# Fourier mixing and an MLP mixer on one core: where the residual adds, the block sums and the edge copies of the second channel product run

## The chip, the cores and the metric

The kernel runs on one NeuronCore of one Trainium2 chip. The metric is the device time of one execution in microseconds. Three runs of the kernel before took 618.13, 616.25 and 618.18 us, with a median of 618.13 us.

## The reference

The input x is 8 batches of 3008 rows and 256 features. It goes through a Fourier mixing (the real part of a two-dimensional FFT over rows and features) and then through a mixer: a two-layer MLP over the rows (256 hidden units) that is added to its input, and a two-layer MLP over the features (1536 hidden units) that is added too.

```
def _attn_ref(x):
    X = np.fft.fft(np.fft.fft(x, axis=1), axis=2)
    return X.real
def _moe_ref(x, w_tok1, w_tok2, w_ch1, w_ch2):
    xt = x.transpose(0, 2, 1)
    h = np.maximum(xt @ w_tok1, 0.0) @ w_tok2
    u = x + h.transpose(0, 2, 1)
    h2 = np.maximum(u @ w_ch1, 0.0) @ w_ch2
    return (u + h2)
```

## The kernel before

**Batches, chunks and quarters.** The outer loop (L772) goes over the 8 batches b. A batch's u lies in SBUF turned (features on partitions) in six chunks of 512 rows (L775, `ut`). Each chunk is worked in four quarters s (L782); I call quarter s of chunk c "sub" 4c+s, 24 to a batch. In a quarter, `mm1` (L584) makes three of the twelve 128-unit tiles of the hidden layer of the present chunk: six matmuls of 512 columns into PSUM `pc`, and three relu copies by ScalarE into `c1` (L595).

**The second channel product.** `mm2` runs one chunk behind: in the same quarter it makes a quarter of the previous chunk's output. For 42 of the 48 chunks this is `mm2_sums` (L620), a product by halves with block sums (a Strassen-like scheme, with seven block products for eight). The other six chunks, "plain" ones (L581), use direct products (L690) and VectorE alone for their residual adds (L702).

In `mm2_sums` two PSUM banks `px` and `py` are kept for a whole chunk, and the four quarters use them in turn:

- s=0: two products from `c1` into `px`; ScalarE copies half of `px` out into `m` (`keep(0)`, L638); VectorE adds the other half and `m` into the output tile `osb` (L645); then GpSimd adds the residual u (tile `rt`) to the same 128x256 part of `osb` (L646).
- s=1: a product of the block sum `sb[0]` into `py`, one of `sb[1]` into `px`, and `keep(1)`.
- s=2: a product of `c1` into `px`, `keep(2)`, and VectorE's add from `py` and `m` (L654). The part of `c1` that it reads has been overwritten by a block sum.
- s=3: a product into `px`, one of `sb[2]` into `py`, two adds by VectorE (L658, L659); then GpSimd adds the residual to the whole upper half of `osb`, 128x512 (L660), and SyncE writes `osb` out in two DMAs (L664).

**Block sums.** `block_sums` (L599) are four adds on VectorE for each half of a chunk's hidden tiles, 128x768 in fp16, all inputs in SBUF: sum 0 makes `sb[0]` from `c1`, sum 1 makes `sb[1]` from `sb[0]` and `c1`, sum 2 overwrites part of `c1` from `c1`, sum 3 makes `sb[2]` from `c1` and `sb[1]`. The first half of a chunk's sums is made in its own quarters s=2 (sums 0 and 1) and s=3 (sums 2 and 3), after that quarter's `mm2` (L792). The second half is made in the next chunk's s=0 and s=1, straight after `mm1` and ahead of everything else of the quarter (L786).

**Residual tile and edges.** `rt` is u turned back by two transposing DMAs on SyncE's queue (L575). `edges` (L611) fixes one or two columns of it, a 128x4 copy each on VectorE, at the start of the chunk's `mm2`.

**What sets the order.** The schedule is written by hand (`manual_schedule`): each engine executes in the order in which the code issues to it. Between the steps, pieces of the next batch's front (`front`, L436: `pz`, `pw`, `pt`, `py`/`pq`, `pu`, all from a ring of three PSUM banks) and of the present batch's own front are taken by the numbers of `plan` and `own_plan` (L765 to L769); the fold of a later batch (L414, adds on VectorE) is taken in at the end of quarters (L811). `load_x` (L122), six DMAs from GpSimd's queue, waits for the last fold step of the batch before. The tile framework puts semaphore waits where one engine reads what another writes.

The lines that matter for the order, in quarter s:

```
                mm1(b, c, c1, range(3 * s, 3 * s + 3))
                if s < 2 and prev is not None and not plain(*prev[0:2]):
                    block_sums(prev[2], pbox["sb"], slice(3, HC), (2 * s, 2 * s + 1))
                take(own, own_plan[b > 0][sub])
                take(nxt, n // 2)
                if prev is not None:
                    mm2(*prev, s, pbox)
                if s >= 2 and not plain(b, c):
                    block_sums(c1, box["sb"], slice(0, 3), (2 * s - 4, 2 * s - 3))
                ...
                take(nxt, n - n // 2)
```

Of the kernel before, what the change touches and what calls it, by code (L numbers as in the profile page):

```python
# [40 lines left out]
def kernel(  # L41
# [9 lines left out]
    nc = tc.nc  # L51
# [17 lines left out]
    def ps_out(name):  # L69
        return psum.tile([P, 512], FP32, tag="o2", name=name, bufs=2)  # L70
# [4 lines left out]
    def dram(t, offset, ap):  # L75
        return bass.AP(tensor=t, offset=offset, ap=ap)
# [84 lines left out]
    for t in (tp, tq):  # L161
        for i in range(2):
            h = slice(64 * i, 64 * i + 64)
            nc.scalar.activation(
                out=t[h, :, 64 - 64 * i:128 - 64 * i],
                in_=pcol[h, :].unsqueeze(2).to_broadcast([64, NG, 64]),
                func=AFT.Copy, scale=0.0)
    nc.scalar.activation(out=w1m[64:128, NG - 1, :],
                         in_=pcol[64:128, :].to_broadcast([64, DTOK]),
# [52 lines left out]
    HC = NCT // 2  # L222
# [184 lines left out]
    def align_w2(j):  # L407
        th, k = j // 4, slice(16 * (j % 4), 16 * (j % 4) + 16)
        copy(0, w2p[:, th, k, 0:NQ], w2v[:, th, k, :])
# [161 lines left out]
    def turn_u(b, c):  # L571

        rt = work.tile([P, 4, D + 16], FP16, tag="rt", name="rt", bufs=4)
        for h in range(2):
            nc.sync.dma_start_transpose(  # L575
                out=rt[:, :, h * P:(h + 1) * P], in_=state[b]["ut"][c][:, h, :])
        return rt
# [3 lines left out]
    def plain(b, c):  # L581
        return (b, c) == (0, 0) or c + 1 == NCH and (b % 2 == 0 or b + 1 == BB)
# [16 lines left out]
    def block_sums(c1, sb, k, which):  # L599
        hi = slice(HC + k.start, HC + k.stop)  # L600
        a11, a21 = c1[:, k, 0:D], c1[:, k, D:CW]
        a12, a22 = c1[:, hi, 0:D], c1[:, hi, D:CW]
        sums = ((sb[:, 0, k], a21, a22, AT.add),
                (sb[:, 1, k], sb[:, 0, k], a11, AT.subtract),
                (a21, a11, a21, AT.subtract),
                (sb[:, 2, k], a12, sb[:, 1, k], AT.subtract))
        for i in which:
            o, x, y, op = sums[i]
            nc.vector.tensor_tensor(out=o, in0=x, in1=y, op=op)  # L609

    def edges(rt, c):  # L611
        for o, i in ((D, 0), (0, P)) if c >= 3 else ((D, P),):
            nc.vector.tensor_copy(out=rt[:, :, o:o + 1], in_=rt[:, :, i:i + 1])

    lower, upper, turned_ = slice(0, P), slice(P, D), slice(D, P, -1)

    def residual(eng, o, x, y):
        eng.tensor_tensor(out=o, in0=x, in1=y, op=AT.add)  # L618

    def mm2_sums(b, c, c1, s, box):  # L620
        if s == 0:
            box["osb"] = work.tile([P, 4, D], FP32, tag="osb", name="osb", bufs=3)
            box["m"] = work.tile([P, 3, 2, P], FP32, tag="m", name="m")
            box["po"] = ps_out("px"), ps_out("py")
            edges(box["rt"], c)
        osb, rt, sb, m = (box[i] for i in ("osb", "rt", "sb", "m"))
        pa, pb = (p[:].rearrange("p (i t d) -> p i t d", i=2, t=2) for p in box["po"])

        def product(o, a, hi, w, first=False):
            for t in range(2):  # L630
                f = D * hi + P * t
                for k in range(HC):
                    nc.tensor.matmul(o[:, t], lhsT=a(k)[:, f:f + P], rhs=w(k),  # L633
                                     start=(first and t == 0 and k == 0),
                                     stop=(k == HC - 1), skip_group_check=True)

        def keep(i):
            nc.scalar.activation(out=m[:, i], in_=pa[:, 0], func=AFT.Copy)  # L638

        v, g = nc.vector, nc.gpsimd  # L640
        if s == 0:
            product(pa[:, 0], lambda k: c1[:, k], 0, lambda k: wc2[:, k, lower], True)
            product(pa[:, 1], lambda k: c1[:, HC + k], 0, lambda k: wc2[:, HC + k, lower])
            keep(0)
            residual(v, osb[:, 0:2, lower], pa[:, 1], m[:, 0])  # L645
            residual(g, osb[:, 0:2, lower], osb[:, 0:2, lower], rt[:, 0:2, lower])  # L646
        elif s == 1:
            product(pb[:, 0], lambda k: sb[:, 0, k], 0, lambda k: wst[:, 0, k], True)
            product(pa[:, 0], lambda k: sb[:, 1, k], 0, lambda k: wst[:, 1, k])
            keep(1)  # L650
        elif s == 2:
            product(pa[:, 0], lambda k: c1[:, k], 1, lambda k: wst[:, 2, k])
            keep(2)
            residual(v, osb[:, 2:4, upper], pb[:, 0], m[:, 2])  # L654
        else:
            product(pa[:, 0], lambda k: c1[:, HC + k], 1, lambda k: wst[:, 3, k])
            product(pb[:, 0], lambda k: sb[:, 2, k], 0, lambda k: wc2[:, HC + k, upper])
            residual(v, osb[:, 2:4, lower], pa[:, 0], rt[:, 2:4, lower])  # L658
            residual(v, osb[:, 0:2, upper], pb[:, 0], m[:, 1])  # L659
            residual(g, osb[:, :, upper], osb[:, :, upper], rt[:, :, turned_])  # L660
        if s == 3:
            for i in range(2):
                nk = 3 if c + 1 == NCH and i else 4
                nc.sync.dma_start(  # L664
                    out=dram(out_t, (b * S + 8 * c + i) * D,
                             [[NQ * D, 64], [2 * D, nk], [1, D]]),
                    in_=osb[64 * i:64 * i + 64, 0:nk, :])
            if c + 1 == NCH:
                nc.sync.dma_start(
                    out=dram(out_t, ((b - 1) * S + NQ - 1) * D, [[NQ * D, 64], [1, D]]),  # L670
                    in_=osb[64:P, 3, :])

    def mm2(b, c, c1, ks, box):
        if not plain(b, c):
            return mm2_sums(b, c, c1, ks, box)
# [41 lines left out]
    def pair(b, c1):  # L717

        if b % 2 == 0 and b + 1 < BB:
            state["ch"] = work.tile([P, NCT, 64], FP16, tag="ch", name="ch")  # L720
            nc.vector.tensor_copy(out=state["ch"][:], in_=c1[:, :, CW - 128:CW - 64])
        elif b % 2:
            nc.vector.tensor_copy(out=c1[:, :, CW - 64:CW], in_=state["ch"][:])


    def take(g, n):
        for _ in range(n):
            next(g, None)
# [41 lines left out]
    prev = None  # L770
    turned_u = {(0, 0): turn_u(0, 0)}
    for b in range(BB):  # L772
        nxt = front(b + 1) if b + 1 < BB else iter(())
        folds = fold(b + 2, [nc.vector] * 4) if b + 2 < BB else None
        for c in range(NCH):  # L775
            c1 = work.tile([P, NCT, CW], FP16, tag="c1", name="c1", bufs=2)
            box = {"rt": turned_u.pop((b, c))}
            if not plain(b, c):
                box["sb"] = work.tile([P, 3, HC, D], FP16, tag="sb", name="sb", bufs=2)
            if c + 1 == NCH and b % 2:  # L780
                pair(b, c1)
            for s in range(4):  # L782
                sub = 4 * c + s
                n = plan[b > 0][sub]
                mm1(b, c, c1, range(3 * s, 3 * s + 3))
                if s < 2 and prev is not None and not plain(*prev[0:2]):  # L786
                    block_sums(prev[2], pbox["sb"], slice(3, HC), (2 * s, 2 * s + 1))
                take(own, own_plan[b > 0][sub])
                take(nxt, n // 2)
                if prev is not None:  # L790
                    mm2(*prev, s, pbox)
                if s >= 2 and not plain(b, c):  # L792
                    block_sums(c1, box["sb"], slice(0, 3), (2 * s - 4, 2 * s - 3))
                if b == 0 and sub < 16 and sub % 2:
                    align_w2(sub // 2)
                take(nxt, n - n // 2)
                if s == 2 and c + 1 < NCH:
                    turned_u[b, c + 1] = turn_u(b, c + 1)
                if s == 3 and c + 1 == NCH and b + 1 < BB:
                    turned_u[b + 1, 0] = turn_u(b + 1, 0)  # L800
                if b == 0 and sub == 4:
                    weight_sums()
                if b == 0 and sub == 3:
                    for h in range(2):
                        swap_wc1(h)
                if b == 0 and 3 <= sub < 9:
                    take(early, 2)
                    if sub == 8:
                        x_tiles[2] = load_x(2)
                if folds is not None and sub >= fold_at[b > 0]:  # L810
                    take(folds, 1 + (b == 0))  # L811
                    if sub == fold_at[b > 0] + (5 if b == 0 else 11) and b + 3 < BB:
                        x_tiles[b + 3] = load_x(b + 3)
            if c + 1 == NCH and b % 2 == 0:
                pair(b, c1)
            prev, pbox = (b, c, c1), box
        own = nxt
# [32 lines left out]
```

## Time and profile before

| what | value |
|---|---|
| median of three runs | 618.13 us |
| the profiled execution's own time | 616.26 us |
| its span, first to last instruction | 614.2 us |
| TensorE matmul (PE) busy | 589.1 us, 96% of the span |
| VectorE (DVE) busy | 492.8 us, 80% |
| ScalarE (ACT) busy | 442.0 us, 72% |
| GpSimd (POOL) busy | 139.3 us, 23% |
| GpSimd's 84 residual adds | 92.2 us |
| granted TensorE clock | 1.0 |

Busy time is the time in which at least one instruction of an engine was executing. A row of a group reads: source line, engine, operation, written tile <- read tiles, shapes, count | busy us, mean ns of one | idle us of the engine just before, and what ended it. A row of the timeline reads: start in us, length in us, engine, line, operation, tiles, shape, count, and in square brackets the idle time ahead of it. Matmul lengths overlap, since matmuls are pipelined: twelve matmuls of 128 columns follow each other in 0.67 us although each is shown with 219 ns. So TensorE's lost time is read from starts: a group should start when the group before it started, plus its count times its pitch.

### The profile page before, as it was taken

How to read it: one execution, taken by the hardware profiler on the slowest of the kernel's cores; microseconds unless marked ns; L12 is line 12 of the kernel's file. 1: busy time of each engine (PE TensorE's matmuls, PEld its weight loads, DVE VectorE, ACT ScalarE, POOL GpSimd, SP SyncE). 2: the span in 40 equal slices, each digit the busy share in tenths (PEclk: the TensorE clock that was granted, in tenths of full speed). 3: DMA queues.
4: the chain of work that ended last, by engine and by line, in shares of the span. 5: the costliest groups of instructions: out<-in, count | busy, mean ns of one | idle time of the engine just before them, and what ended most of it. 6: DMA issues, size and time to landing. Idle time of an engine off the chain costs nothing.

```text
span 614.2 us, 15694 instructions
## 1 busy us (share of the span) xinstructions
PE 589.1 (96%) x6322; PEld 422.5 (69%) x6322; DVE 492.8 (80%) x1086; ACT 442.0 (72%) x996; POOL 139.3 (23%) x163
## 2 busy tenths in 40 slices
PE   2899999999999999999999999999999999999996
PEld 1766767667776767767676777766776767766675
DVE  8768879668998699768988789857899778867684
ACT  8866986677767777686766767777777777667772
POOL 8500413111142121302114221311121212101121
PEclk9999999999999999999999999999999999999999
DMA  8994842725347323672419234392222433232433
GB/s 137 210 192 93 183 67 56 162 57 84 53 89 141 85 52 68 118 120 52 97 44 174 53 83 74 61 183 61 53 62 58 91 53 75 65 69 60 88 62 94
DMA packets 86600, 56.52 MB, mean 92 GB/s; under 512 B 54864, under 2 KB 83472, under 8 KB 85776
## 3 DMA queue, kind: packets, MB, share of 16 engines
q1 hardware_dynamic: 78048, 37.84, 30.9%
q0 software_dynamic: 8256, 17.49, 16.5%
q8 instruction: 49, 0.80, 0.5%
q10 hardware_dynamic: 224, 0.20, 0.1%
q14 instruction: 23, 0.19, 0.1%
HBM read 34.98 MB, written 24.64 MB: 97 GB/s over the span
## 4 chain that ended last, share of the span: by engine, by line
PE 80%; DVE 8%; ACT 6%; issue 3%; POOL 1%; DMA 1%; DVEq 0%; POOLq 0%
PE pc L592 33%; PE px L633 20%; PE py L633 7%; PE pu L552 6%; PE po L690 4%; PE pt L488 3%; ACT c L595 3%; DVE sb L609 2%; DVE osb L618 2%; PE pz L445 1%; PE pw L472 1%; PE pw L473 1%; DVE ut L560 1%; PE py L519 1%; DVE yt L526 1%
## 5 line engine op out<-in xcount | busy, mean ns | idle before, releaser
L595 ACT ACTIVATE c<-pc 128x512 f16<-128x512 f32 (+1 forms) x572 | 295.8, 594 | 39.2 <-PE pc L592 19.8
L618 POOL TENSOR_TENSOR osb<-osb,rt 128x256 f32<-128x256 f32 x84 | 92.2, 1097 | 438.5 <-DVE osb L618 411.4
L592 PE MATMUL pc<-ut,wc1p 128*128 128x512 f16 x576 | 140.3, 379 | 0.0
L592 PE MATMUL pc<-ut,wc1m 128*128 128x512 f16 (+1 forms) x576 | 134.9, 370 | 0.0
L633 PEld LDWEIGHTS <-c 128*128 128x128 f16 x2016 | 121.3, 98 | 19.4 <-issue 0.3
L633 PEld LDWEIGHTS <-sb 128*128 128x128 f16 x1512 | 90.2, 98 | 14.1 <-issue 5.0
L638 ACT ACTIVATE m<-px 128x256 f32<-128x256 f32 x126 | 48.6, 386 | 69.9 <-PE px L633 45.2
L592 PEld LDWEIGHTS <-wc1p 128*128 128x128 f16 x576 | 52.2, 98 | 49.0 <-issue 2.3
L560 DVE TENSOR_TENSOR ut<-pu,yt 128x512 f16<-128x512 f32 (+1 forms) x96 | 64.1, 669 | 26.1 <-PE pu L552 26.1
L592 PEld LDWEIGHTS <-wc1m 128*128 128x128 f16 x576 | 53.0, 98 | 46.3
L609 DVE TENSOR_TENSOR sb<-c,sb 128x768 f16<-128x768 f16 x84 | 84.4, 1004 | 0.0
L633 PE MATMUL px<-wst,c 128*128 128x128 f16 x1008 | 70.0, 219 | 0.0
L633 PE MATMUL px<-wc,c 128*128 128x128 f16 x1008 | 63.1, 219 | 0.0
L618 DVE TENSOR_TENSOR osb<-py,m 128x256 f32<-128x256 f32 x84 | 35.4, 422 | 29.4 <-ACT m L638 23.2
L290 ACT ACTIVATE z<-pz 128x480 f16<-128x480 f32 (+1 forms) x60 | 40.1, 672 | 19.4 <-PE pz L445 12.4
L552 PE MATMUL pu<-w2p,uu 128*128 128x512 f16 (+1 forms) x168 | 50.0, 379 | 0.0
L609 DVE TENSOR_TENSOR c<-c 128x768 f16<-128x768 f16 x84 | 49.5, 590 | 0.0
L609 DVE TENSOR_TENSOR sb<-sb,c 128x768 f16<-128x768 f16 x84 | 46.9, 558 | 2.9
L609 DVE TENSOR_TENSOR sb<-c 128x768 f16<-128x768 f16 x84 | 45.9, 547 | 2.4 <-ACT c L595 2.4
L475 DVE SCALAR_TENSOR_TENSOR w<-alt,pw 128x131 f16<-128x131 f16 x96 | 33.0, 350 | 14.4 <-ACT w L290 14.3
L633 PE MATMUL px<-wst,sb 128*128 128x128 f16 x504 | 34.9, 219 | 3.2 <-DVE osb L618 2.6
L526 DVE TENSOR_TENSOR yt<-py,qs 128x512 f16<-128x512 f32 x48 | 30.8, 683 | 8.8 <-ACT qs L522 8.8
(163 smaller groups left out, 674.3 us busy)
## 6 DMA issues: line engine op xcount, KB each, us to landing
out_dram<-osb SPq DMA_DIRECT2D x83, 256.0 KB, 3.7
xp<-in_x_dram POOLq DMA_DIRECT2D x16, 272.0 KB
out_dram<-osb SPq DMA_DIRECT2D x11, 192.0 KB, 3.2
xp<-in_x_dram POOLq DMA_DIRECT2D x16, 127.5 KB
rt<-ut SPq DMA_TRANSPOSE x96, 3.4
w2s<-in_moe_w_tok_dram POOLq DMA_DIRECT2D x1, 1504.0 KB
w1p<-in_moe_w_tok_dram POOLq DMA_DIRECT2D x2, 384.0 KB
wc<-in_moe_w_ch_dram POOLq DMA_DIRECT2D x1, 768.0 KB
```

Of the source, the lines that this page charges most:

```text
L290: nc.scalar.activation(out=out_, in_=in_, func=AFT.Copy)
L475: nc.vector.scalar_tensor_tensor(out=w[:, g, 0:131], in0=alt[:], scalar=pw[:, 131:132], in1=pw[:, 0:131], op0=AT.mult, op1=AT.add)
L526: nc.vector.tensor_tensor(out=yt[:, h, CW * c:CW * c + CW], in0=py[:], in1=qs[:], op=op)
L552: nc.tensor.matmul(pu[:, 0:n], lhsT=uu[:, th, int(minus), h, :], rhs=w2_cols(b, c)[:, th], start=(th == 0), stop=(th == 1))
L560: nc.vector.tensor_tensor(out=ut[:, h, 0:n].rearrange("p (a b) -> p a b", b=64), in0=pu[:, 0:n].rearrange("p (b a) -> p a b", b=64), in1=y ...
L592: nc.tensor.matmul(pc[:, 0:n], lhsT=wc[:, h, ct * P:(ct + 1) * P], rhs=ut[:, h, 0:n], start=(h == 0), stop=(h == 1))
L595: nc.scalar.activation(out=c1[:, ct, 0:n], in_=pc[:, 0:n], func=AFT.Relu)
L609: nc.vector.tensor_tensor(out=o, in0=x, in1=y, op=op)
L618: eng.tensor_tensor(out=o, in0=x, in1=y, op=AT.add)
L633: nc.tensor.matmul(o[:, t], lhsT=a(k)[:, f:f + P], rhs=w(k), start=(first and t == 0 and k == 0), stop=(k == HC - 1), skip_group_check=True)
L638: nc.scalar.activation(out=m[:, i], in_=pa[:, 0], func=AFT.Copy)
L690: nc.tensor.matmul(po[0:n, o:o + D], lhsT=c1[:, ct, ks * P:ks * P + n], rhs=wc2[:, ct, :], start=(ct == 0), stop=(ct == NCT - 1))
```

## The change

Three things change.

1. The two residual adds of a chunk that GpSimd made (L646 and L660) are made by VectorE: `g` becomes `nc.vector`.
2. The edge copies (L613) go from VectorE to GpSimd.
3. The block sums are issued at other places of the quarter. In s=0 (second half, sums 0 and 1) they come after the first pieces of the fronts, just ahead of `mm2`. In s=1 (second half, sums 2 and 3) they come last, after `mm2` and the remaining pieces of the front. In s=2 (first half, sums 0 and 1) they stay behind `mm2`. In s=3 (first half, sums 2 and 3) they come straight after `mm1`, ahead of `mm2`.

```
     def edges(rt, c):
         for o, i in ((D, 0), (0, P)) if c >= 3 else ((D, P),):
-            nc.vector.tensor_copy(out=rt[:, :, o:o + 1], in_=rt[:, :, i:i + 1])
+            nc.gpsimd.tensor_copy(out=rt[:, :, o:o + 1], in_=rt[:, :, i:i + 1])
...
-        v, g = nc.vector, nc.gpsimd
+        v, g = nc.vector, nc.vector
...
                 mm1(b, c, c1, range(3 * s, 3 * s + 3))
-                if s < 2 and prev is not None and not plain(*prev[0:2]):
-                    block_sums(prev[2], pbox["sb"], slice(3, HC), (2 * s, 2 * s + 1))
+                def now():
+                    which = 2 * (s % 2), 2 * (s % 2) + 1
+                    if s >= 2 and not plain(b, c):
+                        block_sums(c1, box["sb"], slice(0, 3), which)
+                    elif s < 2 and prev is not None and not plain(*prev[0:2]):
+                        block_sums(prev[2], pbox["sb"], slice(3, HC), which)
+
+                if s == 3:
+                    now()
                 take(own, own_plan[b > 0][sub])
                 take(nxt, n // 2)
+                if s == 0:
+                    now()
                 if prev is not None:
                     mm2(*prev, s, pbox)
-                if s >= 2 and not plain(b, c):
-                    block_sums(c1, box["sb"], slice(0, 3), (2 * s - 4, 2 * s - 3))
+                if s == 2:
+                    now()
                 if b == 0 and sub < 16 and sub % 2:
                     align_w2(sub // 2)
                 take(nxt, n - n // 2)
+                if s == 1:
+                    now()
```

The instructions of TensorE, ScalarE and SyncE, and their order, are the same in both kernels. GpSimd keeps its setup work and its DMA issues, loses 84 adds and gains 72 copies; VectorE gains the 84 adds and loses the 72 copies.

## Prediction

> **What bounds the kernel now.** I read the page first: engine shares and the chain that ended last.
>
> ```profile
> PE 589.1 (96%) x6322; PEld 422.5 (69%) x6322; DVE 492.8 (80%) x1086; ACT 442.0 (72%) x996; POOL 139.3 (23%) x163
> ...
> PE 80%; DVE 8%; ACT 6%; issue 3%; POOL 1%; DMA 1%; DVEq 0%; POOLq 0%
> ```
>
> TensorE is busy nearly all the time and makes 80% of the chain; VectorE makes 8% and ScalarE 6%, the places where TensorE had to wait. Next, who TensorE waited for:
>
> ```profile
> PE px L633 <- DVE osb L618: 2.6, 8, 0.8
> PE pz L445 <- DVE ut L560: 1.6, 3, 0.7
> PE pt L488 <- DVE w L475: 1.1, 1, 1.1
> ```
>
> The columns are us in total, times, longest. These count only idle time between modelled ends. To size the real stalls I went through all matmuls in order of start and compared each start-to-start distance with the pitch of undisturbed groups (12 products of 128 columns in 0.67 us, six of 512 in 1.29 us). After 60 us, distances more than 0.06 us too long add up to 13.6 us. Of these `px<-wst,sb` (the second product of quarter s=1) has 5.6 us in 15 places, `pz` 2.1 us in 3, `pt<-w` 1.95 us in 7. The other 3.9 us are mostly small matmuls of L455 to L461, which have nothing to do with the change. So VectorE can give back 9.7 us at most. Before 60 us and after the last matmul nothing of the change lies.
>
> What makes VectorE late shows in the timeline around one such place:
>
> ```profile
> 312.62 0.55 DVE L609 TENSOR_TENSOR c<-c 128x768 f16<-128x768 f16 x1
> 312.79 1.41 POOL L618 TENSOR_TENSOR osb<-osb,rt 128x512 f32<-128x512 f32 x1 [7.00 <-DVE osb L618]
> 313.09 1.52 DVE L609 TENSOR_TENSOR sb<-c,sb 128x768 f16<-128x768 f16 x1
> ...
> 317.94 0.83 PE L633 MATMUL py<-wst,sb 128*128 128x128 f16 x12
> 318.12 0.38 DVE L613 COPY rt<-rt 128x4 f16<-128x4 f16 x2
> 318.85 0.42 DVE L618 TENSOR_TENSOR osb<-px,m 128x256 f32<-128x256 f32 x1 [0.35 <-ACT c L595]
> ...
> 319.33 0.83 PE L633 MATMUL px<-wst,sb 128*128 128x128 f16 x12 [0.56 <-DVE osb L618]
> ```
>
> GpSimd's 128x512 add runs from 312.79 to 314.20, and VectorE's block sum beside it takes 1.52 us. Five us later `py` starts at 317.94 and is due to end its issue at 317.94 + 0.67 = 318.61, but `px<-wst,sb` starts at 319.33: it waits for the add at 318.85 that reads the same bank, and that add stands behind block sums and edge copies in VectorE's queue. The groups by shape tell how much time goes this way:
>
> ```profile
> L609 DVE TENSOR_TENSOR sb<-c,sb 128x768 f16<-128x768 f16 x84 | 84.4, 1004 | 0.0
> L609 DVE TENSOR_TENSOR c<-c 128x768 f16<-128x768 f16 x84 | 49.5, 590 | 0.0
> L609 DVE TENSOR_TENSOR sb<-sb,c 128x768 f16<-128x768 f16 x84 | 46.9, 558 | 2.9
> L609 DVE TENSOR_TENSOR sb<-c 128x768 f16<-128x768 f16 x84 | 45.9, 547 | 2.4 <-ACT c L595 2.4
> ...
> L613 DVE COPY rt<-rt 128x4 f16<-128x4 f16 x72 | 13.3, 184 | 0.8
> ...
> L245 DVE TENSOR_TENSOR gr<-gv,mp 128x768 f32<-128x768 f32 x1 | 1.0, 959 | 0.0
> ...
> L245 DVE TENSOR_TENSOR gr<-gv,m 94x120 f32<-94x120 f32 x1 | 0.3, 280 | 0.0
> ```
>
> ```profile
> L618 POOL TENSOR_TENSOR osb<-osb,rt 128x512 f32<-128x512 f32 x42 | 60.3, 1437 | 241.8 <-DVE osb L618 237.1 <-DVE rt L613 4.7
> L618 POOL TENSOR_TENSOR osb<-osb,rt 128x256 f32<-128x256 f32 x42 | 31.8, 758 | 196.6 <-DVE osb L618 174.3 <-DMA out_dram<-osb 22.3
> ```
>
> The four block sums have the same shape and type, but take 547, 558, 590 and 1004 ns. Instruction by instruction, VectorE operations after 45 us are 53.8 us longer than the undisturbed ones of their shape: 38.5 us in `sb<-c,sb`, 3.6 in `c<-c`, 9.7 in the fold, the rest in copies. Every one of them overlaps a GpSimd residual add.
>
> [...] block sums (both inputs in SBUF) are stretched by 1.0 us, the adds from PSUM (423 ns) never. [...]
>
> **The change, part by part.**
>
> Adds to VectorE: 42 of 256 and 42 of 512 elements, both inputs in SBUF, not shown in the trace on this engine. Between the L245 rows (120 elements 280 ns, 768 elements 959) the slope is 1.05 ns, so 0.42 and 0.69 us[...]. Lower bound 0.41 and 0.68 (the same sizes from PSUM, L618 and L560), upper 0.45 and 0.72 with the 0.034 us seen ahead of an operation that waits for its forerunner. Sum 42 x 1.11 = 46.6 us of VectorE. The s=0 add stands behind the add that TensorE waits for, the s=3 add behind both adds that free `px` and `py`. It delays what follows: front pieces and the next sums.
>
> Adds off GpSimd: the 53.8 us of contention go. Edge copies off VectorE: 72 x 0.184 = 13.3 us. VectorE: 492.8 + 46.6 - 53.8 - 13.3 = 472 us. Little in sum; what counts is where. At the end of s=3, behind the adds from PSUM, stood sum 2 (0.55) and a sum 3 of 0.55 to 2.04 us; now the 0.69 us add stands there, and the two sums run ahead, while TensorE still makes the products that those adds await. VectorE enters s=0 about 1.3 us earlier where there was contention, and its queue to the critical add is 0.17 to 0.38 us of copies shorter.
>
> I followed the stretch above with measured durations, queued operations 0.08 us closer than their length, as in the timeline. Sums 2 and 3 end by 311.84, the adds from PSUM by 312.7, the residual add at 313.3 (before, sum 3 at 314.61). The two `yt` operations wait for ScalarE's `qs` (315.99) and end at 317.3; two sums end at 318.3, the critical add at 318.62. `py` issues until 318.61, so `px` waits about 0.1 us, not 0.72. Likewise at 329.98, where `pz` loses 0.88 us behind a sum of 2.04 us, `ut` ends at 328.45 and `pz` is due at 328.5. So I leave 0.8 of the 5.6 us, 0.4 of the 2.1 and 0.85 of the 1.95: in the `pt` case at 97.39 the last `w` now stands behind the 0.69 us add, not behind 1.1 us of sums. Gain 4.8 + 1.7 + 1.1 = 7.6 us.
>
> New wait one: in s=1 sum 2 (`c<-c`) now comes last, and the product of s=2 needs it from its fourth weight on. Where a `w` or `ut` of the same quarter stands ahead of it, it can't start early. That holds in 13 chunks with `w` (subs 9 and 17 of six batches, and one of the first) and about 7 with `ut` (sub 21). At 306.5 ScalarE's `w` ends 306.52, VectorE's `w` takes to 306.9, `c<-c` 306.83 to 307.37; the fourth weight is due at 307.22 + 3 x 0.058 = 307.40. Just late; at 285.4 the same sum gives 0.08 us late. I take 0.1 us x 13 = 1.3 us; the `ut` case has 0.07 us to spare in the stretch above. Bounds: 0 and 0.3 us each, 0 to 6 us. Behind the waiting matmul stands all of TensorE.
>
> New wait two: VectorE's s=0 add waits for GpSimd's edge copies, and behind it stands all of VectorE. GpSimd now does little else, so the copies run as soon as `rt` lands, chunks ahead. The exception is behind `load_x`: at the two batch boundaries after 60 us where block sums follow, its issues end at 183.25 and 327.70, and the next critical add at 188.5 and 332.9. About 5 us to spare, for two copies: nothing. If that cover were gone, those places would lose what is missing, one for one.
>
> Edge copies on GpSimd: its rows on 128x1 tiles last 0.19 to 0.64 us, so 72 cost 14 to 46 us of an idle engine. [...] I take 0.2 us and nothing on the path, the other end is rival B. SyncE's output DMAs wait for an add that ends 0.9 us earlier; nothing is queued longer.
>
> Sum: 7.6 - 1.3 = 6.3 us. Against the profiled execution, 616.26 - 6.3 = 610.0 (span 607.9). The median of the runs lies 1.9 us above that execution (two runs at 618.1, one at 616.25), so for the median **618.13 - 6.3 = 611.8 us**.
>
> **The rivals.**
>
> B, [...] After the change two-input VectorE work is 185 us of sums, 47 of adds and 52 of fold, 46% of the span. 72 copies of 0.64 us would block 21 us. Before, 53.8 us blocked cost at most 9.7, under a fifth: 3.8 us. Time 611.8 + 3.8 = 615.6. For it: a copy was itself stretched to 1.16 us beside a GpSimd add, so the engines do collide. Against: four elements a partition are a tenth of the add's work or less.
>
> C, slower: sum 2 is late. Its place at the end of s=1, the 20 chunks above, is the mechanism; the price is the lateness of `c<-c` to TensorE, in full. For it: the working above has no margin. Against: it is late by hundredths when the queue ahead is empty. It decides from 7.6 / 20 = 0.38 us each: there the gain is used up (618). If VectorE brings a backlog of its own into these quarters, say 0.75 us each, it is 618.1 - 7.6 + 15 = 625.5 us.
>
> That the change doesn't do what it says is ruled out by the order of instructions, which shows 84 adds and 72 copies on their new engines, TensorE's order untouched.
>
> **How the numbers follow.** Forecast 0.60 (608 to 614.5; from lateness 0 to 0.3 us and 0 to 4 us of the old stalls left), B 0.17 (614.5 to 617), C 0.23, of which 0.06 end within 0.3% (up to 619) and 0.17 above. 0.3% of 618.13 is 1.9 us, about what this measurement can tell from no change. B splits at 616.3 into 0.10 faster, 0.07 same. So faster 0.70, same 0.13, slower 0.17. The range 608 to 618.5 holds the forecast, B and C's small end.
>
> **What would show it.** Right: `sb<-c,sb` at 0.55 us, VectorE 472 us busy, `px<-wst,sb` stalls below 1 us, TensorE's excess after 60 us near 7 us. Wrong: `px<-wst,c` waiting for VectorE's `c` in subs 10, 18 and 22 (C); two-input operations of VectorE still stretched, beside edge copies (B); VectorE idle until GpSimd's `rt` at batch boundaries.

## The result, and the profile after

The changed kernel takes 611.87 us (median of four runs, 611.84 to 613.79), the kernel before 617.82 us beside it. The ratio is 0.9916, with a 95% interval of 0.9890 to 0.9942: faster by 0.6% to 1.1%. The profiled execution took 611.84 us, with a span of 610.1 us.

**The spread of the traces comes from the set-up.** Both kernels' times lie between a lowest value and some 2 us above it (before: 616.25 to 618.18). The traces of all kernels of this study show where: the first `pc` matmul starts at 38.4 us in some executions and as late as 40.5 us in others, whatever the kernel. The two lines below, from the changed kernel and from run `e10_one_w_first`, show the same 24 `filler` matmuls of L283:

```profile
21.41 1.50 PE L283 MATMUL filler<-anti,ident 128*128 128x128 f16 x24
```

```profile
22.18 2.76 PE L283 MATMUL filler<-anti,ident 128*128 128x128 f16 x24
```

From start to start they take 0.056 us each in the first trace and 0.107 us in the second.

So beside the ratio I use the time from the first `pc` matmul to the end of the trace, the main part, which is free of this: 575.8 us before, 571.6 us after, 4.1 us less. Up to the first place that an edit reaches, 48.5 us into the main part, the matmuls of all 13 traces of this study start within 0.003 us of each other. The profiled executions differ by 4.4 us (616.26 and 611.84), of which 0.3 us lies outside the span: 616.26 - 614.2 = 2.1 us before, 611.84 - 610.1 = 1.7 us after.

The page of the changed kernel, engine shares and chain:

```profile
PE 587.2 (96%) x6322; PEld 420.8 (69%) x6322; DVE 478.0 (78%) x1098; ACT 442.3 (72%) x996; POOL 66.6 (11%) x151
...
PE 83%; DVE 2%; issue 0%; DVEq 0%
```

These shares add up to only 85%, because the chain is followed back no further than 88.1 us here; in the kernel before it goes back into the set-up, so the two lists can't be compared as they stand. From 88.2 us on, VectorE makes 35.0 us of the chain before and 9.5 us after, ScalarE 25.5 us and none, and from 98 us on VectorE makes 0.3 us: there TensorE alone holds the end. Who TensorE still waited for (us in total, times, longest):

```profile
PE pt L488 <- DVE w L475: 1.4, 1, 1.4
...
PE py L633 <- DVE sb L609: 0.3, 1, 0.3
...
PE px L633 <- DVE osb L618: 0.2, 1, 0.2
PE px L633 <- DVE c L609: 0.2, 1, 0.2
```

The 2.6 us of `px` behind the add from PSUM have gone down to 0.2, `pz` behind `ut` is gone; one wait of `pt` for the last `w` is left, 1.4 us long, and has grown from 1.1. (Waits of the set-up are left out.) Measured as in the prediction, start to start, TensorE's excess after 60 us fell from 13.6 to 9.1 us: `px<-wst,sb` 5.6 to 1.35, `pz` 2.1 to 0, `pt<-w` 1.95 to 2.4, and two that were not there, `px<-wst,c` 1.4 in 12 places and one `py<-wst,sb` of 0.47. The excess fell by 4.5 us and the main part by 4.1; the rest is in delays of 0.06 us or less, which the excess doesn't count.

The stretch that the prediction followed, in the trace after (start us, us, engine, line, operation, tiles, shape, count):

```profile
309.46 0.55 DVE L609 TENSOR_TENSOR c<-c 128x768 f16<-128x768 f16 x1
309.93 0.55 DVE L609 TENSOR_TENSOR sb<-c,sb 128x768 f16<-128x768 f16 x1
...
310.40 0.41 DVE L618 TENSOR_TENSOR osb<-px,rt 128x256 f32<-128x256 f32 x1
...
310.92 0.42 DVE L618 TENSOR_TENSOR osb<-py,m 128x256 f32<-128x256 f32 x1
311.38 0.70 DVE L618 TENSOR_TENSOR osb<-osb,rt 128x512 f32<-128x512 f32 x1
...
314.66 1.29 DVE L526 TENSOR_TENSOR yt<-py,qs 128x512 f16<-128x512 f32 x2 [0.65 <-ACT qs L522]
...
315.87 0.55 DVE L609 TENSOR_TENSOR sb<-c 128x768 f16<-128x768 f16 x1
...
316.45 0.56 DVE L609 TENSOR_TENSOR sb<-sb,c 128x768 f16<-128x768 f16 x1
316.57 0.83 PE L633 MATMUL py<-wst,sb 128*128 128x128 f16 x12
316.93 0.42 DVE L618 TENSOR_TENSOR osb<-px,m 128x256 f32<-128x256 f32 x1
317.40 0.83 PE L633 MATMUL px<-wst,sb 128*128 128x128 f16 x12
```

Sums 2 and 3 now run back to back, 0.55 us each, ahead of the adds from PSUM; the residual add ends at 312.08, and VectorE then waits 0.52 us for ScalarE. `py` starts at 316.57 and issues until 317.24; the critical add ends at 317.35; `px` starts at 317.40, 0.16 us late instead of 0.72. But look at 314.66: VectorE had waited 0.65 us there for ScalarE's `qs`, with the two sums queued behind `yt`. The groups by shape:

```profile
L609 DVE TENSOR_TENSOR sb<-sb,c 128x768 f16<-128x768 f16 x84 | 46.9, 558 | 2.9
L609 DVE TENSOR_TENSOR sb<-c,sb 128x768 f16<-128x768 f16 x84 | 46.2, 550 | 0.0
L609 DVE TENSOR_TENSOR sb<-c 128x768 f16<-128x768 f16 x84 | 46.2, 550 | 2.3 <-ACT c L595 2.3
L609 DVE TENSOR_TENSOR c<-c 128x768 f16<-128x768 f16 x84 | 46.1, 548 | 0.0
...
L618 DVE TENSOR_TENSOR osb<-osb,rt 128x512 f32<-128x512 f32 x42 | 29.1, 693 | 3.1 <-issue 0.4
...
L618 DVE TENSOR_TENSOR osb<-osb,rt 128x256 f32<-128x256 f32 x42 | 17.9, 425 | 2.5
```

```profile
L613 POOL COPY rt<-rt 128x4 f16<-128x4 f16 x72 | 19.6, 273 | 373.4 <-DMA rt<-ut 302.2 <-DVE osb L618 50.8 <-DVE eo L429 10.0
```

All four sums take 548 to 558 ns. The two adds take 425 and 693 ns, where 0.42 and 0.69 us were forecast; the copies 273 ns on GpSimd.

### The profile page after: what moved, and what is told of

It is laid out like the page before. It is cut to its first block, busy times and chain, and to the rows that moved or that the text cites. A ratio compares the mean times of both kernels' runs of the same rounds, so it can differ in the third digit from the quotient of the medians.

```text
span 610.1 us, 15679 instructions
## 1 busy us (share of the span) xinstructions
PE 587.2 (96%) x6322; PEld 420.8 (69%) x6322; DVE 478.0 (78%) x1098; ACT 442.3 (72%) x996; POOL 66.6 (11%) x151
## 4 chain that ended last, share of the span: by engine, by line
PE 83%; DVE 2%; issue 0%; DVEq 0%
PE pc L592 36%; PE px L633 22%; PE py L633 9%; PE pu L552 6%; PE po L690 3%; PE pt L488 3%; PE pz L445 1%; PE pq L519 1%; PE py L519 1%; PE pw L473 1%; PE pw L472 1%; DVE osb L618 0%; DVE sb L609 0%; DVE w L475 0%; PE pz L461 0%; PE pz L455 0%
## 5 line engine op out<-in xcount | busy, mean ns | idle before, releaser
L638 ACT ACTIVATE m<-px 128x256 f32<-128x256 f32 x126 | 48.5, 385 | 66.8 <-PE px L633 42.4
L633 PE MATMUL px<-wst,c 128*128 128x128 f16 x1008 | 71.3, 220 | 0.2 <-DVE c L609 0.2
L613 POOL COPY rt<-rt 128x4 f16<-128x4 f16 x72 | 19.6, 273 | 373.4 <-DMA rt<-ut 302.2
L618 DVE TENSOR_TENSOR osb<-osb,rt 128x256 f32<-128x256 f32 x84 | 47.0, 559 | 5.6 <-issue 0.4
L609 DVE TENSOR_TENSOR sb<-c,sb 128x768 f16<-128x768 f16 x84 | 46.2, 550 | 0.0
L609 DVE TENSOR_TENSOR c<-c 128x768 f16<-128x768 f16 x84 | 46.1, 548 | 0.0
## 6 DMA issues: line engine op xcount, KB each, us to landing
w2s<-in_moe_w_tok_dram POOLq DMA_DIRECT2D x1, 1504.0 KB, 17.9
```

The source lines that it names most:

```text
L613: nc.gpsimd.tensor_copy(out=rt[:, :, o:o + 1], in_=rt[:, :, i:i + 1])
L633: nc.tensor.matmul(o[:, t], lhsT=a(k)[:, f:f + P], rhs=w(k), start=(first and t == 0 and k == 0), stop=(k == HC - 1), skip_group_check=True)
```

## The experiments

All are measured beside the kernel before, on the same chip within a group. Each group has its own runs of the kernel before (medians of 616.4 to 617.6 us), to which its ratios refer; the row "before" has the result's. Excess is TensorE's, after 60 us. "Main" is the main part. "Lowest" is the lowest of a kernel's runs.

| run | median us | lowest us | ratio to before, 95% interval | main, us | excess, us | VectorE busy, us |
|---|---|---|---|---|---|---|
| before | 617.8 | 616.25 | 1 | 575.8 | 13.6 | 492.8 |
| changed kernel | 611.9 | 611.84 | 0.9916 (0.9890 to 0.9942) | 571.6 | 9.1 | 478.0 |
| e1_adds_only | 611.9 | 611.23 | 0.9920 (0.9901 to 0.9938) | 570.9 | 8.5 | 485.7 |
| e2_sums_only | 617.1 | 615.26 | 0.9984 (0.9975 to 0.9994) | 574.8 | 12.4 | 466.3 |
| e3_edges_back | 614.6 | 614.37 | 0.9971 (0.9958 to 0.9983) | 574.1 | 11.5 | 486.3 |
| e4_sums_back | 610.1 | 609.76 | 0.9889 (0.9871 to 0.9907) | 569.6 | 7.2 | 477.4 |
| e5_sum2_early | 612.6 | 611.17 | 0.9917 (0.9899 to 0.9934) | 571.0 | 8.7 | 477.6 |
| e6_pool_reads | 624.2 | 623.00 | 1.0114 (1.0096 to 1.0132) | 582.8 | 20.2 | 507.5 |
| e7_pool_writes | 613.0 | 612.39 | 0.9930 (0.9913 to 0.9947) | 572.2 | 9.3 | 478.6 |
| e9_front_first | 613.6 | 613.44 | 0.9945 (0.9928 to 0.9961) | 573.3 | 10.9 | 475.1 |
| e10_one_w_first | 609.3 | 609.28 | 0.9884 (0.9866 to 0.9901) | 569.1 | 6.8 | 477.2 |
| e11_s0_first | 611.3 | 610.58 | 0.9911 (0.9896 to 0.9927) | 570.4 | 8.0 | 477.7 |
| e12_s3_ahead | 611.1 | 609.99 | 0.9906 (0.9891 to 0.9921) | 569.8 | 7.4 | 475.1 |

The theory at the start: GpSimd's adds blocked VectorE, so the adds' move makes the gain (theory 1). The rivals: the new places of the sums make it (theory 2), or the copies' removal from VectorE does (theory 3).

### e1: the adds alone

```
-        v, g = nc.vector, nc.gpsimd
+        v, g = nc.vector, nc.vector
```

> Only the adds move to VectorE; block sums and edge copies stay where they were. Theory 1 [...]: sums 2 and 3 all at 0.55 us, VectorE busy 492.8 - 53.8 + 46.6 = 486 us, most of the gain is there, 613 to 615 us. Theory 2 (the new places of the sums make the gain): nothing gained, since VectorE's queue behind the s=3 adds even grows by 0.69 us, 617 to 620 us.

Measured: 611.9 us, better than theory 1 had it, and VectorE 485.7 us busy as computed (486). The adds' move gives 4.8 us of the main part, more than the whole change. Theory 2 falls: VectorE's queue behind the s=3 adds is 0.69 us longer here, and still the time falls.

### e2: the sums alone

The changed kernel with both other edits undone (`g` on GpSimd, edge copies on VectorE).

> Only the block sums are re-placed; GpSimd keeps its adds, VectorE the edge copies. Theory 1: the blocking goes on, only against other operations (sums 0 and 1, fold), VectorE stays near 490 us busy, 615.5 to 618 us. Theory 2: nearly the whole gain, 612 to 613 us.

Measured: 617.1 us, 1.0 us of the main part. As theory 1 has it in time, but VectorE is 466 us busy, not 490: operations are stretched by about 24.6 us only, instead of 53.8. The trace shows why: 111 block sums overlap a GpSimd residual add in the kernel before and 16 here, while the operations from PSUM that overlap one (`w`, `ut`, `yt`) go from 33 to 55. In the kernel before, the 25 `w` and 8 `ut` among them take 342 to 350 and 678 to 692 ns, no longer than the others of their shape (342 to 359 and 675 to 693). The prediction's adds from PSUM into `osb` say nothing here: none of the 196 overlaps a GpSimd add. More than half of the blocked time went without TensorE gaining much: `px<-wst,sb` has 6.2 us of stalls, before 5.6. So the sum of blocked time isn't the price; its place is.

### e3: the edge copies back on VectorE

```
-            nc.gpsimd.tensor_copy(out=rt[:, :, o:o + 1], ...)
+            nc.vector.tensor_copy(out=rt[:, :, o:o + 1], ...)
```

> The changed kernel with the edge copies back on VectorE. Theory 1: 72 copies of 0.17 us (12 us of VectorE) stand ahead of the s=0 add that TensorE waits for, but VectorE has spare time there in most chunks: 612 to 613.5 us. Theory 3 (the copies' removal from the queue ahead of the critical add is a main part): 614 us or more.

Measured: 614.6 us, as theory 3 has it: 2.5 us of the main part, for 8.3 us of VectorE's busy time. The copies stand right ahead of the critical add, and TensorE's wait for it is back:

```profile
PE px L633 <- DVE osb L618: 3.0, 10, 0.6
```

With the sums at their old places the same edit is worth 1.4 us (e1 against e4). So the copies' move is a real part of the gain, and its worth depends on how tight the sums stand.

### e4: the sums back at their old places

The kernel before, with the edits of adds and copies only.

> Adds on VectorE and edge copies on GpSimd, block sums at their old places. Theory 1: no blocking, a queue 1.1 us longer behind the s=3 adds than in the changed kernel, but no late sum 2 in s=1 (1.4 us of stalls less): 612 to 614 us. Theory 2: no gain, 616 to 619 us.

Measured: 610.1 us, below what theory 1 had expected; 2.1 us of the main part better than the changed kernel. **The re-placement of the sums costs time once the adds are on VectorE.** The prediction had counted it as a gain.

### e5, e11, e12: which of the sums' new places costs

e5 issues sums 2 and 3 of s=1 ahead of the last front piece; e11 issues sums 0 and 1 of s=0 first in the quarter; e12 takes e4 and moves only the sums of s=3 ahead of the products.

```
+                if s == 1:
+                    now()
                 take(nxt, n - n // 2)
-                if s == 1:
-                    now()
```

```
-                if s == 3:
+                if s == 3 or s == 0:
                     now()
                 take(own, own_plan[b > 0][sub])
                 take(nxt, n // 2)
-                if s == 0:
-                    now()
```

```
+                if s == 3 and not plain(b, c):
+                    block_sums(c1, box["sb"], slice(0, 3), (2, 3))
                 take(own, own_plan[b > 0][sub])
...
-                if s >= 2 and not plain(b, c):
+                if s == 2 and not plain(b, c):
```

> The changed kernel, but in s=1 sums 2 and 3 are issued ahead of the last front piece of the quarter instead of behind it. If the stalls of px<-wst,c in the changed kernel (1.4 us in 12 places) come from sum 2 standing behind w, they go: about 610.5 us. If they only reflect a VectorE that is late anyway, they stay and the time stays near 611.9 us.

> The changed kernel, with sums 0 and 1 of s=0 back ahead of the front pieces. If these sums, queued behind yt which waits for ScalarE, are what the re-placement costs, the px<-wst,sb stalls (1.35 us) and the py one (0.47 us) mostly go: 610.5 us. If s=1 and s=3 cost it, 611.9 us.

> Adds on VectorE, edge copies on GpSimd, all sums at their old places but those of s=3, which go ahead of the products as in the changed kernel. If running them ahead helps as the prediction says, pt<-w in the first batch loses 0.4 us or more of its 2.0 us and px<-wst,sb stays below 1 us: 609 to 610 us. If it hurts (the adds from PSUM come later), above 611 us.

Measured on the main part: the place in s=0 costs 571.6 - 570.4 = 1.2 us, that in s=1 571.6 - 571.0 = 0.7 us, that in s=3 569.8 - 569.6 = 0.2 us; together 2.1 us, the difference between e4 and the changed kernel. Each is a difference of two single traces, but the lowest runs give the same: 611.84 - 610.58 = 1.3 us, 611.84 - 611.17 = 0.7 us, 609.99 - 609.76 = 0.2 us. (The medians of e5, e11 and e12 hold executions with early and with late set-ups, 611.2 to 613.3 for e5, and would not separate them; they lie 2.1, 0.8 and 1.1 us above what was expected if the edit helped.) In e5 the 1.4 us of `px<-wst,c` fall to 0.1, so the late sum 2 was as real as forecast; about half of it came back as short waits of `pu`, `px` and `pt`. In e11 the stalls that were to go mostly went only in part: `px<-wst,sb` falls from 1.35 to 0.9, `py<-wst,sb` from 0.47 to 0.2, and `px<-wst,c` from 1.4 to 0.9. In e12 running the sums ahead in s=3 doesn't help: of the 2.0 us in one place of the first batch 0.4 goes, but as much comes up at the `w` before it, and `pt<-w` stays at 2.7 us in all. The stretch of e11 that answers to the one above:

```profile
313.49 0.55 DVE L609 TENSOR_TENSOR sb<-c 128x768 f16<-128x768 f16 x1
...
314.07 0.56 DVE L609 TENSOR_TENSOR sb<-sb,c 128x768 f16<-128x768 f16 x1
314.55 1.28 DVE L526 TENSOR_TENSOR yt<-py,qs 128x512 f16<-128x512 f32 x2
...
315.75 0.42 DVE L618 TENSOR_TENSOR osb<-px,m 128x256 f32<-128x256 f32 x1
316.13 0.83 PE L633 MATMUL py<-wst,sb 128*128 128x128 f16 x12
...
316.80 0.83 PE L633 MATMUL px<-wst,sb 128*128 128x128 f16 x12
```

The two sums now run while VectorE would wait for `qs`; `yt` starts with no idle time ahead of it. The critical add runs from 315.75 to 316.17; `py` starts at 316.13 and issues its matmuls until about 316.80, and `px` starts then, not late at all.

### e6 and e7: GpSimd reads again, or only writes

e6 is the changed kernel, and after each of the two adds GpSimd repeats it into a scratch tile; e7 puts a memset of that tile there. The output and VectorE's and TensorE's work are those of the changed kernel. The edit of e6 in s=3:

```
             residual(g, osb[:, :, upper], osb[:, :, upper], rt[:, :, turned_])
+            scr = work.tile([P, 4, P], FP32, tag="scr", name="scr")
+            residual(nc.gpsimd, scr[:], osb[:, :, upper], rt[:, :, turned_])
```

> The changed kernel, and GpSimd repeats both residual adds into a scratch tile that nobody reads: VectorE and TensorE have the same work as in the changed kernel. Theory 1 [...]: two-input VectorE operations are stretched again by 20 us or more, TensorE's stalls return, 614 to 622 us. If it was the place of the adds [...]: 612 us, sums at 0.55 us.

> The same with a memset of the same scratch tile in place of each of GpSimd's adds: GpSimd is busy but reads nothing from SBUF. Theory 1 with reads as the cause: VectorE's sums stay at 0.55 us, 612 us. If any work of GpSimd holds VectorE up: sums stretched as with the reading adds, above 614 us.

Measured: 624.2 us with the reads, 11.2 us of the main part; 613.0 us with the writes, 0.6 us of the main part, of which 0.5 us lies behind the last matmul (5.32 us from there to the end, 4.85 in the changed kernel). In e6 operations of VectorE are stretched by 28.7 us, all beside a GpSimd add. Two places, GpSimd's add and VectorE's operation:

```profile
295.67 1.16 POOL L618 TENSOR_TENSOR scr<-osb,rt 128x512 f32<-128x512 f32 x1 [8.50 <-DVE osb L618]
295.71 1.41 DVE L429 TENSOR_TENSOR eo<-xp 94x512 f16<-94x512 f16 x1
...
299.74 0.67 POOL L618 TENSOR_TENSOR scr<-osb,rt 128x256 f32<-128x256 f32 x1 [2.56 <-issue]
299.79 0.90 DVE L431 TENSOR_TENSOR eo<-xp 94x508 f16<-94x508 f16 x1
```

The operations of L429 and L431, 0.42 us each when alone, end 0.29 and 0.28 us after GpSimd's add has ended. That GpSimd keeps tiles which VectorE needs is no rival here: after 45 us VectorE waits for GpSimd only once, 1.7 us for an edge copy at 614.35 us, and the time from the last matmul to the end is 4.84 us, as in the changed kernel. TensorE's excess is 20.2 us, 11.1 more than in the changed kernel; its largest listed waits for VectorE:

```profile
PE px L633 <- DVE osb L618: 2.7, 11, 0.2
PE py L633 <- DVE sb L609: 2.1, 6, 1.3
PE pt L488 <- DVE w L475: 1.4, 1, 1.4
PE px L633 <- DVE c L609: 1.4, 3, 0.6
```

In e7 GpSimd has these memsets, and VectorE's sum stays at its own length:

```profile
L664 POOL MEMSET scr<- 128x512 f32 x42 | 22.3, 531 | 2.1
...
L648 POOL MEMSET scr<- 128x256 f32 x42 | 13.0, 309 | 0.0
```

```profile
L609 DVE TENSOR_TENSOR sb<-c,sb 128x768 f16<-128x768 f16 x84 | 46.3, 551 | 0.0
```

So GpSimd's adds, which read SBUF, stretch VectorE's operations by 28.7 us in e6, and its memsets, which only write, leave the block sums as they are: 36 of them run beside a memset in e7, and none is longer by more than 0.04 us. The copies into `ch` (one input, 128x768 fp16) do not stay as they are: two of the four run beside a memset and take 618 and 620 ns, the other two 350 and 351. That GpSimd's adds hold VectorE up and make TensorE wait, as theory 1 has it, is shown; by what means, no run shows.

### e9 and e10: the last stall of the first batch

In e4 one wait of 2.0 us is left in the first batch, where TensorE needs the last `w` and VectorE has the upper residual add and two sums ahead of it. e9 issues the last front piece of each s=2 and s=3 ahead of sums, upper add and output; e10 does so in sub 19 of the first batch alone; its edit, the core of it:

```
                 finish = mm2(*prev, s, pbox) if prev is not None else None
+                held = b == 0 and sub == 19
+                if held:
+                    take(nxt, n - n // 2)
                 if finish is not None:
                     finish()
```

> Adds on VectorE, edge copies on GpSimd, block sums of s=0 and s=1 at their old places; in s=2 and s=3 the last front piece is issued ahead of the block sums and of the upper residual add with its output DMAs. In the run with the sums back, 2.0 of 2.7 us of pt<-w stalls stood in one place of the first batch, where the last w waits behind the upper add and two sums (0.69 + 0.55 + 0.47 us). If that is their cause they shrink by 1.7 us: 608.4 us. If VectorE's backlog of folds there is the cause: 610 us.

> The kernel with adds on VectorE, edge copies on GpSimd and all block sums at their old places; only in sub 19 of the first batch the last w is issued ahead of the upper residual add and sums 2 and 3. The 2.0 us stall of pt<-w there should fall to about 0.35 us and nothing else change: TensorE's excess after 60 us 7.2 - 1.7 = 5.5 us, about 608.5 us. If VectorE's backlog there passes to the next wait instead, 610 us.

Measured: e9 613.6 us, against both expectations; e10 609.3 us, between its two. TensorE's waits in e9, then in e10:

```profile
PE px L633 <- DVE osb L618: 3.7, 6, 0.8
...
PE pt L488 <- DVE w L475: 0.2, 1, 0.2
```

```profile
PE px L633 <- DVE osb L618: 0.5, 1, 0.5
...
PE pt L488 <- DVE w L475: 0.2, 1, 0.2
```

The `pt` wait goes in both (0.2 us shown, 0.37 us start to start). In e9 the sums of s=2 and s=3 come later in every chunk, and reach the critical add of s=0: 4.8 us of `px<-wst,sb` stalls. In e10 1.15 us of the 1.7 come back a few us later as waits of `pu` and `py`, so VectorE's backlog there, with the folds of two batches, is mostly passed on. e10 has the lowest main part of all, 569.1 us, and e4 the next, 569.6 us. Both beat the changed kernel there by 2.1 to 2.6 us; their lowest runs by 2.1 and 2.6 us too. Their ratios to before are lower as well, but the intervals overlap with the changed kernel's.

## Why the prediction was right, and where not

**The total.** Forecast 611.8 us, measured 611.87. That they agree so closely is luck. The sum was 6.3 us; the main part fell by 4.1 us, and the profiled executions by 616.26 - 611.84 = 4.4 us. The medians differ by more, 618.13 - 611.87 = 6.3 us (6.0 us with the fourth run before), because the first median (618.13, of 616.25, 618.13 and 618.18) lies at the upper end of the runs' spread and the second (611.87, of 611.84 twice, 611.89 and 613.79) at the lower. That the timed runs spread because of the set-up, as the traces do, is inferred. The prediction subtracted a difference read from traces from a median at the upper end.

**What bounds the kernel.** Right: TensorE's waits for VectorE, at most 9.7 us. The terms, with what was to be left: `px<-wst,sb` 0.8, measured 1.35; `pz` 0.4, measured 0; `pt<-w` 0.85, measured 2.4.

**The step that failed** is the one on `pt<-w`, that the last `w` "now stands behind the 0.69 us add, not behind 1.1 us of sums". The place before and after:

```profile
96.06 0.54 DVE L609 TENSOR_TENSOR c<-c 128x768 f16<-128x768 f16 x1
...
96.52 0.55 DVE L609 TENSOR_TENSOR sb<-c,sb 128x768 f16<-128x768 f16 x1
96.99 0.35 DVE L475 SCALAR_TENSOR_TENSOR w<-alt,pw 128x131 f16<-128x131 f16 x1
...
97.39 0.22 PE L488 MATMUL pt<-w,hp 128*128 128x130 f16 x1 [1.12 <-DVE w L475]
```

```profile
94.89 0.54 DVE L609 TENSOR_TENSOR c<-c 128x768 f16<-128x768 f16 x1
...
95.36 0.55 DVE L609 TENSOR_TENSOR sb<-c,sb 128x768 f16<-128x768 f16 x1
...
96.87 0.69 DVE L618 TENSOR_TENSOR osb<-osb,rt 128x512 f32<-128x512 f32 x1
97.48 0.35 DVE L475 SCALAR_TENSOR_TENSOR w<-alt,pw 128x131 f16<-128x131 f16 x1
...
97.88 0.22 PE L488 MATMUL pt<-w,hp 128*128 128x130 f16 x1 [1.44 <-DVE w L475]
```

The sums that run ahead are still ahead of the last `w`: VectorE was behind at that place, not waiting for TensorE, so nothing of them was hidden and the add came on top. The `w` starts 0.49 us later, and the stall grew from 1.28 to 1.60 us, start to start. (And by the reason given, 0.69 us in place of 1.1, only 0.4 us would have gone, not the 1.1 us that the sum took for `pt<-w`.) This term is 1.55 of the 2.2 us by which the sum was too high. More widely, the prediction took the new places of the sums for a gain; e4 shows that they cost 2.1 us, most of it in s=0, where they wait behind `yt` (e11). The gain came from the adds and the copies.

**Price of the adds.** Right: 0.42 and 0.69 us each, 29.1 + 17.9 = 47.0 us together, where the forecast was 46.6. VectorE's total was forecast at 472 us and is 478: the copies' 13.3 us were a sum of lengths, but they overlap their neighbours, and their move frees only 8.3 us (486.3 in e3 against 478.0).

**New wait one, the late sum 2.** Right in mechanism and size: 1.3 us forecast in 13 places, 1.4 in 12 measured. Rival C, that VectorE's backlog makes it large, did not come.

**New wait two, VectorE behind the edge copies.** Right: no such wait is listed for VectorE.

**Rival B, the edge copies hold VectorE up.** Refuted: VectorE's operations after 45 us are longer than undisturbed by 0.1 us in all. A GpSimd copy took 273 ns, not 0.2 us.

**What was undervalued.** The copies' move counted as 0.17 to 0.38 us of queue ahead of the critical add, with no term of its own. It is worth 2.5 us in the changed kernel (e3).

## What to carry to other kernels

Work that GpSimd took over from VectorE wasn't free here: 84 small adds stretched VectorE's operations by 53.8 us, 51.8 us of it in two-input ones, more than the 47.0 us that VectorE needs to make the adds itself. What that cost the kernel depended on the place and not on the sum (29.2 us less of it gained 1.0 us in e2): look at what is queued ahead of the one VectorE operation that TensorE waits for, and don't put work that is ready behind an operation that still waits for another engine (1.2 us in e11). Before a gain read from traces is subtracted from a median, it pays to see where the runs' own spread arises.

## What the runs showed of the hardware that was not expected

The set-up's matmuls of 128 columns go over from 0.107 to 0.056 us each at different times: between 18.7 and 21.4 us in the trace before, between 13.7 and 18.0 in the one after, later than 22.2 in e10. In the traces where the slow pace still holds after 22 us (e2, e4, e5, e7, e10) the first `pc` matmul starts at 39.6 to 40.5 us, in all others at 38.4. What sets that time is open: the granted clock is listed as 1.00 for the four `filler` matmuls at 18.40 us before, which take 0.106 us each, and as 1.00 for the same four at 17.97 us after, which take 0.056. And 28.7 us of blocked VectorE time cost 11.2 us where VectorE also has the adds (e6), while the kernel before lost no more than 9.7 us to 53.8 us.

Copies with one input were held up beside GpSimd too: in the kernel before, two copies into `ch` took 844 and 848 ns beside a residual add, the other two 350 and 351.
